# First expert stage: activations become the matmul weights, and the layout is put right by 32x32 transposes and a finer reload

## The chip, the cores and the metric

The kernel runs on one core of a Trainium2 chip. The time is device microseconds (us) of one execution, from runs on the chip; a profiled execution shows what each engine did. TensorE is called PE in the rows (PEld is its loading of weights), VectorE is DVE, ScalarE is ACT, GpSimd is POOL, and SP is SyncE, whose queue issues all the transfers of this kernel.

## The reference, cut to what matters

A gated linear recurrence over 4 batches, 8 heads, 768 steps and head size 40 gives 3072 tokens of 320 features. Two expert layers follow:

```
x = attn_out.transpose(0, 2, 1, 3).reshape(3072, 320)
h = maximum(x @ w1_in, 0);   x2  = (h * h) @ w1_out      # 320 -> 2048 -> 320
h = x2 @ w2_in;              out = (h * sigmoid(h)) @ w2_out
```

Inputs and output are float32. The kernel keeps that precision by splitting each factor into a high part and a low remainder and adding three products: high x high, high x low, low x high.

## The kernel before, in words

**Stages.** Stage 1 is the first expert layer in 8 blocks of 384 tokens (n = 0 to 7), with the recurrence (24 tiles of 128 tokens) woven in between; from the last blocks on it is alone. Stage 2 is the second layer in 6 blocks of 512 tokens. Each block has 16 steps j, one for each 128 of the 2048 hidden features. "Out step (n, j)" below is the second product of step j in block n, and "in step (n, j)" the first; blocks of stage 2 are n = 8 to 13.

**A step.** `in_mm` makes the hidden features with 8 matmuls into the PSUM tile `hin` (two buffers). ACT and DVE turn that into `gh` (high part) and `gl` (low part), 128 features by the tokens of the block. `emit_out` adds the second product into the PSUM tiles `o0`, `o1`, `o2` (and `o3` in stage 2), which have one buffer each, so the next block's out step 0 can't start until they have been copied out. In steps run three steps ahead of out steps (`AHEAD`).

**The two ways of the second product.** In stage 1 the weights `wo` are loaded into PE and `gh` and `gl` stream past: the result has features in rows and tokens in columns, which is what stage 2's first product needs. The 320 features are cut in 128, 128 and 64; the last 64 are laid beside their low parts, so that 8 matmuls of 384 columns do the step (lines 764 to 773). The two halves of the last tile are added later by POOL (line 811). In stage 2 `gh` and `gl` are loaded as the weights, 128 tokens at a time, and `wo` (320 columns) streams: 3 matmuls for each 128 tokens (lines 783 to 785).

**Between the stages.** ACT, DVE and ACT copy `o0`, `o1`, `o2` to `ob` (lines 776 to 778), and one transfer writes it to `x2_d` in DRAM. `x2_load` reads a block of 512 tokens back into `xr` (two buffers), in 5 transfers (lines 801 and 804), and `x2_split` makes the high part on ACT (line 812) and the low part on DVE (line 813). The first load is asked for at the start of block 7. In block 7 the weights of stage 2 are read back as well, 640 KB at a time (`w2_take`: `wi0`, `wo0`, `wi1`, ...), each when stage 1 is done with that weight tile.

**Order.** Block 0 follows a written table (`ORDER`). In blocks 1 to 7 the order of the code is the order on PE, ACT, DVE and SP. From block 8 on only PE's order is that of the code; the framework's own simulation places that work of the others, some of it (block 9's reload) in among block 7's, so a change of tiles moves it on ACT, DVE and SP. Each of these works through its list strictly in order: an instruction that waits holds up all behind it.

Of the kernel before, what the change touches and what calls it, by code (L numbers as in the profile page):

```python
# [8 lines left out]
F32 = mybir.dt.float32  # L9
F32R = mybir.dt.float32r  # L10
# [101 lines left out]
def f(ap):  # L112
    return ap.bitcast(F32)
# [7 lines left out]
def mlstm_moe_kernel(  # L121
# [32 lines left out]

    g_d = dram.tile([B * H, S], F32, name="g_d")
    e_d = dram.tile([B * H, S], F32, name="e_d")
    x2_d = dram.tile([128, 3, NT], F32, name="x2_d")
    w2_d = {(k, u): dram.tile([128, 1280], F32, name=f"w2{k}{u}_d") for u in range(8) for k in "io"}


# [112 lines left out]
    def w_split(raw, which, layer, u, pl):  # L273
        n = 768 if which == "i" else 640
        lo, hi = raw[:, :, 0], raw[:, :, 1]
        t = pl.tile([128, 768], I32, tag="dt", name="dt", bufs=DT_BUFS)[:, 0:n]
        act.activation(out=f(t), in_=f(hi), func=ACTF.Prelu, scale=2.0 ** -112, alpha=-2.0 ** 32)
        yield
        dve.tensor_scalar(out=t, in0=t, scalar1=3, scalar2=None, op0=ALU.logical_shift_left)
        dve.scalar_tensor_tensor(out=t, in0=lo, scalar=29, in1=t,  # L280
                                 op0=ALU.logical_shift_right, op1=ALU.bitwise_or)
        yield
        if which == "i":
            if layer == 1:
# [11 lines left out]
        elif layer == 1:  # L296
            w = wout[layer, u] = wp.tile([128, 2, 640], F32R, tag=f"wo{u}", name=f"wo{u}")
            tv = f(t).rearrange("p (j n) -> p j n", j=2)
            parts = ((slice(0, 256), slice(0, 256), slice(256, 512)),
                     (slice(256, 320), slice(512, 576), slice(576, 640)))  # L300
            for c, oh, ol in parts:
                act.activation(out=w[:, :, oh], in_=tv[:, :, c], func=ACTF.Copy)
            yield
            for c, oh, ol in parts:
                (pool if PLAN.get(f"@Mo{u}", 1) else dve).tensor_tensor(out=w[:, :, ol], in0=tv[:, :, c], in1=f(w[:, :, oh]), op=ALU.subtract)  # L305
        else:
            ws = pl.tile([128, 1280], F32R, tag="raw", name="ws", bufs=RAW_BUFS)
            w = ws.rearrange("p (j n) -> p j n", j=2)
# [443 lines left out]
    def emit_out(bi, j):  # L752
# [6 lines left out]
                O[bi].append(p_at.tile([128, 512], F32, tag="at", name="o3"))  # L759
        o = O[bi]  # L760
        first, last = j == 0, j == KF - 1
        if ly == 1:
            for k in range(2):
                c = slice(k * 128, k * 128 + 128)
                c2 = slice(256 + k * 128, 256 + k * 128 + 128)
                pe.matmul(o[k][:, 0:N], w[:, c], gh, start=first, stop=False)  # L766
                pe.matmul(o[k][:, 0:N], w[:, c2], gh, start=False, stop=False)  # L767
                pe.matmul(o[k][:, 0:N], w[:, c], gl, start=False, stop=last)  # L768
            if first:
                pe.matmul(o[2][:, 0:N], w[:, 512:640], gh, start=True, stop=False)  # L770
            pe.matmul(o[2][0:64, 0:N], w[:, 512:576], gl, start=False, stop=False)  # L771
            if not first:
                pe.matmul(o[2][:, 0:N], w[:, 512:640], gh, start=False, stop=last)  # L773
            if last:
                ob = stp.tile([128, 3, NMAX], F32, tag="raw", name="ob", bufs=RAW_BUFS)
                act.activation(out=ob[:, 0, 0:N], in_=o[0][:, 0:N], func=ACTF.Copy)
                dve.tensor_copy(out=ob[:, 1, 0:N], in_=o[1][:, 0:N])
                act.activation(out=ob[:, 2, 0:N], in_=o[2][:, 0:N], func=ACTF.Copy)
                late.append(lambda: sp.dma_start(out=x2_d[:, :, t0:t0 + N], in_=ob[:, :, 0:N]))
        else:  # L780
            for k in range(N // 128):
                c = slice(k * 128, k * 128 + 128)
                pe.matmul(o[k][:, 0:DM], gh[:, c], w[:, 0:320], start=first, stop=False)  # L783
                pe.matmul(o[k][:, 0:DM], gh[:, c], w[:, 320:640], start=False, stop=False)  # L784
                pe.matmul(o[k][:, 0:DM], gl[:, c], w[:, 0:320], start=False, stop=last)  # L785
            if last:
                ob = mp.tile([128, 4, DM], F32, tag="ob", name="ob")
                for k in range(N // 128):
                    if k % 2 == 0:
                        act.activation(out=ob[:, k], in_=o[k][:, 0:DM], func=ACTF.Copy)  # L790
                    else:
                        dve.tensor_copy(out=ob[:, k], in_=o[k][:, 0:DM])
                    b, c = TILES[t0 // L + k]
                    r0 = b * S + c * L
                    sp.dma_start(out=out[r0:r0 + L, :], in_=ob[:, k])

    def x2_load(n):
        ly, _, t0, N = blocks[len(BLK1) + n]
        xr = ph2.tile([128, 4, NMAX2], F32, tag="xr", name="xr", bufs=2)[:, :, 0:N]
        c = slice(t0, t0 + N)  # L800
        sp.dma_start(out=xr[:, 0:2], in_=x2_d[:, 0:2, c])
        for s in range(2):
            for p in range(2):
                sp.dma_start(out=xr[64 * p:64 * p + 64, 2 + s], in_=x2_d[64 * s:64 * s + 64, 2, c])
        return xr

    def x2_split(n, xr):
# [328 lines left out]
```

## Time and profile before

| | |
|---|---|
| median of 3 runs | 836.83 us (836.72 to 837.45) |
| profiled execution, its own time | 836.38 us |
| span of the profiled execution, first to last instruction | 834.7 us |
| PE busy | 828.2 us (99%) |
| DVE busy, ACT busy | 498.6 us (60%), 493.5 us (59%) |
| granted TensorE clock, mean | 0.999 |

The profiled execution lies 0.45 us below the median, and 1.7 us of it are outside the span. A matmul's busy time in the rows is longer than the distance to the next one's start, because matmuls are pipelined; what a group of matmuls costs is read from starts.

### The profile page before, as it was taken

What the parts mean: (1) busy time and instruction counts of PE and PEld (TensorE: products, weight loads), DVE (VectorE), ACT (ScalarE), POOL (GpSimd) and SP (SyncE); (2) the same over time, 40 slices, a digit from 0 to 9 for tenths busy, and PEclk for the clock granted to TensorE, in tenths of its full rate; (3) what the DMA queues carried; (4) which work ended last, traced back from release to release, by engine and by line L of the source; (5) the groups of instructions that cost most, each with busy time, mean ns of one, the idle gap of its engine ahead of it and who ended that gap; (6) DMA issues with size and microseconds to landing.
All of it is one profiled execution on the core that took longest, in us unless ns stands there. A gap on an engine that the chain in (4) does not pass through costs nothing.

```text
span 834.7 us, 14812 instructions
## 1 busy us (share of the span) xinstructions
PE 828.2 (99%) x5657; PEld 772.1 (92%) x5657; DVE 498.6 (60%) x904; ACT 493.5 (59%) x969; POOL 76.7 (9%) x102
## 2 busy tenths in 40 slices
PE   9999999999999999999999999999999999999998
PEld 5788999999999999999999989999999999999997
DVE  4689988687878776878843253443443533533433
ACT  4688877786977869779656653433333433433332
POOL 3242441100100000001000010000000000000000
PEclk9999999999999999999999999999999999999999
DMA  6777655667777668687511991020100000000000
GB/s 241 224 235 263 188 157 159 209 206 241 236 250 225 209 220 251 196 246 242 185 64 49 355 333 59 6 77 1 51 32 0 33 1 1 32 1 1 33 1 31
DMA packets 69454, 115.68 MB, mean 139 GB/s; under 512 B 5615, under 2 KB 47479, under 8 KB 69383
## 3 DMA queue, kind: packets, MB, share of 16 engines
q1 hardware_dynamic: 69383, 114.74, 42.8%
q8 instruction: 44, 0.72, 0.4%
q14 instruction: 27, 0.22, 0.1%
HBM read 75.48 MB, written 19.33 MB: 114 GB/s over the span
## 4 chain that ended last, share of the span: by engine, by line
PE 94%; DMA 2%; ACT 2%; SPq 1%; DVE 1%; issue 1%
PE hin L711 41%; PE o L785 7%; PE o L784 7%; PE o L783 7%; PE o L766 5%; PE o L767 5%; PE o L768 5%; PE o L771 3%; PE o L773 2%; PE hA L578 2%; PE sc L491 2%; PE hA L563 2%; PE st L613 1%; PE hA L573 1%; PE xT L647 1%; PE sc L485 1%
## 5 line engine op out<-in xcount | busy, mean ns | idle before, releaser
L711 PE MATMUL hin<-x,wi 128*128 128x384 f32 (+1 forms) x1792 | 395.2, 362 | 0.1
L711 PEld LDWEIGHTS hin<-x,wi 128*128 128x128 f32 x1792 | 320.9, 188 | 26.3 <-DVE wi L294 0.4
L742 DVE TENSOR_TENSOR gl<-r,gh 128x384 fp32r<-128x384 f32 (+1 forms) x224 | 140.3, 632 | 96.2 <-ACT gh L728 58.7
L728 ACT ACTIVATE gh<-r 128x384 fp32r<-128x384 f32 (+1 forms) x224 | 127.7, 571 | 69.9 <-DVE r L724 66.1
L724 DVE TENSOR_TENSOR r<-hin,r 128x512 f32<-128x512 f32 x96 | 66.4, 692 | 134.2 <-ACT r L723 134.2
L723 ACT ACTIVATE r<-hin 128x512 f32<-128x512 f32 x96 | 57.3, 597 | 144.8 <-PE hin L711 144.7
L785 PE MATMUL o<-wo,gl 128*128 128x320 f32 x384 | 118.7, 309 | 0.0
L784 PE MATMUL o<-wo,gh 128*128 128x320 f32 x384 | 118.5, 309 | 0.0
L783 PE MATMUL o<-wo,gh 128*128 128x320 f32 x384 | 118.2, 308 | 0.0
L721 ACT ACTIVATE r<-hin 128x384 f32<-128x384 f32 x128 | 62.0, 485 | 84.8 <-PE hin L711 80.9
L766 PE MATMUL o<-gh,wo 128*128 128x384 f32 x256 | 87.9, 343 | 0.0
L767 PE MATMUL o<-gh,wo 128*128 128x384 f32 x256 | 86.5, 338 | 0.0
L768 PE MATMUL o<-gl,wo 128*128 128x384 f32 x256 | 86.5, 338 | 0.0
L783 PEld LDWEIGHTS o<-wo,gh 128*128 128x128 f32 x384 | 72.1, 188 | 3.6
L784 PEld LDWEIGHTS o<-wo,gh 128*128 128x128 f32 x384 | 72.1, 188 | 3.6
L785 PEld LDWEIGHTS o<-wo,gl 128*128 128x128 f32 x384 | 72.1, 188 | 0.0
L736 ACT ACTIVATE r<-r 128x384 f32<-128x384 f32 x126 | 66.2, 525 | 3.8
L455 POOL TENSOR_SCALAR_AFFINE_SELECT W<-W 128x512 f32<-128x512 f32 x42 | 33.0, 807 | 262.8 <-DMA W<-g_d 96.0
L466 ACT ACTIVATE W<-W,aw 128x128 f32<-128x128 f32 x168 | 52.9, 389 | 0.1
L766 PEld LDWEIGHTS o<-gh,wo 128*128 128x128 f32 x256 | 48.1, 188 | 0.4 <-issue 0.2
L767 PEld LDWEIGHTS o<-gh,wo 128*128 128x128 f32 x256 | 48.1, 188 | 0.4 <-POOL wo L305 0.3
L768 PEld LDWEIGHTS o<-gl,wo 128*128 128x128 f32 x256 | 48.1, 188 | 0.0
(151 smaller groups left out, 995.9 us busy)
## 6 DMA issues: line engine op xcount, KB each, us to landing
stk<-tt SPq DMA_DIRECT2D x162, 120.0 KB
raw<-in_w_in_dram SPq DMA_DIRECT2D x16, 768.0 KB
W<-g_d SPq DMA_DIRECT2D x21, 512.0 KB
vk<-in_vk_dram SPq DMA_DIRECT2D x23, 328.0 KB
rqk<-in_qk_dram SPq DMA_DIRECT2D x18, 360.0 KB
ro<-in_w_out_dram SPq DMA_DIRECT2D x8, 640.0 KB
w2i_d<-ws SPq DMA_DIRECT2D x8, 640.0 KB
raw<-in_w_out_dram SPq DMA_DIRECT2D x8, 640.0 KB
```

The costliest lines, as they stand in the source:

```text
L711: pe.matmul(ps[:, 0:N], w[:, c, ws], x[:, sl, 0:N], start=(k == 0), stop=(k == 7))
L721: act.activation(out=r, in_=ps, func=ACTF.Relu)
L724: dve.tensor_tensor(out=r, in0=ps, in1=r, op=ALU.mult)
L728: act.activation(out=gh, in_=r, func=ACTF.Square if blocks[bi][0] == 1 else ACTF.Copy)
L736: act.activation(out=r, in_=r, func=ACTF.Square)
L742: on("gl" if ly == 1 else "gl2", gi).tensor_tensor(out=gl, in0=r, in1=f(gh), op=ALU.subtract)
L766: pe.matmul(o[k][:, 0:N], w[:, c], gh, start=first, stop=False)
L767: pe.matmul(o[k][:, 0:N], w[:, c2], gh, start=False, stop=False)
L768: pe.matmul(o[k][:, 0:N], w[:, c], gl, start=False, stop=last)
L783: pe.matmul(o[k][:, 0:DM], gh[:, c], w[:, 0:320], start=first, stop=False)
L784: pe.matmul(o[k][:, 0:DM], gh[:, c], w[:, 320:640], start=False, stop=False)
L785: pe.matmul(o[k][:, 0:DM], gl[:, c], w[:, 0:320], start=False, stop=last)
```

## The change: what it does

Stage 1's second product is now done as in stage 2: `gh` and `gl` are the weights, and `wo` streams with 320 columns, 9 matmuls for each out step of 384 tokens. The result has tokens in rows. At the end of a block three DVE instructions transpose each 32x32 block of `o0`, `o1`, `o2` on the way to `ob`. Three transfers write `ob` to `x2_d`, which now holds, for each 32 tokens, 32 rows of 320. The reload puts the blocks in their places with 12 transfers for each 512 tokens, each of 32 partitions by 16 pieces of 32 numbers (128 bytes); features 256 to 319 are read twice, as before. POOL's addition is gone. Stage 1's `w_out` is split with one ACT and one POOL or DVE instruction in place of two each.

```
-        if ly == 1:
-            for k in range(2):
-                c = slice(k * 128, k * 128 + 128)
-                c2 = slice(256 + k * 128, 256 + k * 128 + 128)
-                pe.matmul(o[k][:, 0:N], w[:, c], gh, start=first, stop=False)
-                pe.matmul(o[k][:, 0:N], w[:, c2], gh, start=False, stop=False)
-                pe.matmul(o[k][:, 0:N], w[:, c], gl, start=False, stop=last)
...
-                act.activation(out=ob[:, 0, 0:N], in_=o[0][:, 0:N], func=ACTF.Copy)
-                dve.tensor_copy(out=ob[:, 1, 0:N], in_=o[1][:, 0:N])
-                act.activation(out=ob[:, 2, 0:N], in_=o[2][:, 0:N], func=ACTF.Copy)
-                late.append(lambda: sp.dma_start(out=x2_d[:, :, t0:t0 + N], in_=ob[:, :, 0:N]))
...
+        for k in range(N // 128):
+            c = slice(k * 128, k * 128 + 128)
+            pe.matmul(o[k][:, 0:DM], gh[:, c], w[:, 0:320], start=first, stop=False)
+            pe.matmul(o[k][:, 0:DM], gh[:, c], w[:, 320:640], start=False, stop=False)
+            pe.matmul(o[k][:, 0:DM], gl[:, c], w[:, 0:320], start=False, stop=last)
+        if last and ly == 1:
+            ob = stp.tile([128, 3, NMAX], F32, tag="raw", name="ob", bufs=RAW_BUFS)
             for k in range(N // 128):
+                dve.transpose(out=ob[:, k, 0:DM], in_=o[k][:, 0:DM])
+            s0 = t0 // 32
+            late.append(lambda: [sp.dma_start(out=x2_d[s0 + 4 * k:s0 + 4 * k + 4].rearrange("s r d -> (s r) d"), in_=ob[:, k, 0:DM])
+                                 for k in range(N // 128)])
...
     def x2_load(n):
         ly, _, t0, N = blocks[len(BLK1) + n]
-        xr = ph2.tile([128, 4, NMAX2], F32, tag="xr", name="xr", bufs=2)[:, :, 0:N]
-        c = slice(t0, t0 + N)
-        sp.dma_start(out=xr[:, 0:2], in_=x2_d[:, 0:2, c])
-        for s in range(2):
-            for p in range(2):
-                sp.dma_start(out=xr[64 * p:64 * p + 64, 2 + s], in_=x2_d[64 * s:64 * s + 64, 2, c])
+        xr = ph2.tile([128, 3, NMAX2], F32, tag="xr", name="xr", bufs=2)[:, :, 0:N]
+        src = x2_d[t0 // 32:(t0 + N) // 32].rearrange("s r (b c) -> b r s c", c=32)
+        for k in range(12):
+            b = k if k < 10 else k - 2
+            p = 32 * (k % 4)
+            sp.dma_start(out=xr[p:p + 32, k // 4].rearrange("r (s c) -> r s c", c=32), in_=src[b])
         return xr
...
-        on("x2r").tensor_tensor(out=xr[:, 2], in0=xr[:, 2], in1=xr[:, 3], op=ALU.add)
-        act.activation(out=x[:, 0:3], in_=xr[:, 0:3], func=ACTF.Copy)
-        on("x2lo").tensor_tensor(out=x[:, 3:6], in0=xr[:, 0:3], in1=f(x[:, 0:3]), op=ALU.subtract)
+        act.activation(out=x[:, 0:3], in_=xr, func=ACTF.Copy)
+        on("x2lo").tensor_tensor(out=x[:, 3:6], in0=xr, in1=f(x[:, 0:3]), op=ALU.subtract)
```

The placing of stage 2's work moves with it. On SP's queue before, from the first reload (`xr_6323`, block 8's tokens) to the middle of the second one (`xr_6822`, block 9's); line numbers are those of each kernel's own file:

```order
L801 DMA xr_6323<-x2_d_86 128x2x512
L804 DMA xr_6323<-x2_d_86 64x512 x4
L316 DMA w2o7_d_102<-ws_6276 128x1280
L321 DMA wi0_6357<-w2i0_d_87 128x1280
L779 DMA x2_d_86<-ob_6311 384x1x384
...
L321 DMA wi2_6462<-w2i2_d_91 128x1280
L801 DMA xr_6822<-x2_d_86 128x2x512
L804 DMA xr_6822<-x2_d_86 64x512 x2
L324 DMA wo2_6488<-w2o2_d_92 128x1280
L321 DMA wi3_6514<-w2i3_d_93 128x1280
L804 DMA xr_6822<-x2_d_86 64x512 x2
```

And the same stretch of SP's queue now, where `xr_6431` and `xr_6956` are these two reloads:

```order
L785 DMA xr_6431<-x2_d_86 32x16x32 x12
L309 DMA w2o7_d_102<-ws_6382 128x1280
L314 DMA wi0_6473<-w2i0_d_87 128x1280
L765 DMA x2_d_86<-ob_6419 128x320 x3
...
L314 DMA wi3_6638<-w2i3_d_93 128x1280
L785 DMA xr_6956<-x2_d_86 32x16x32 x4
L317 DMA wo3_6665<-w2o3_d_94 128x1280
L314 DMA wi4_6692<-w2i4_d_95 128x1280
L785 DMA xr_6956<-x2_d_86 32x16x32 x8
```

A reload has 12 transfers in place of 5, and the last pieces of block 9's stand behind two more weight transfers, `wo3` and `wi4`.

On DVE at the end of block 7, before (`x_6996` is block 9's low part; `r` and `gl` of 512 columns belong to block 8; `ob_6752` is the copy of block 7's result):

```order
L813 TENSOR_TENSOR x_6996<-xr_6822,x_6996 128x1536
L724 TENSOR_TENSOR r_6687<-hin_6676,r_6687 128x512
L742 TENSOR_TENSOR gl_6660<-r_6661,gh_6659 128x384
L724 TENSOR_TENSOR r_6713<-hin_6702,r_6713 128x512
L742 TENSOR_TENSOR gl_6686<-r_6687,gh_6685 128x512
L724 TENSOR_TENSOR r_6739<-hin_6728,r_6739 128x512
L742 TENSOR_TENSOR gl_6712<-r_6713,gh_6711 128x512
L777 COPY ob_6752<-o1_6347 128x384
```

And DVE at the same place now:

```order
L717 TENSOR_TENSOR r_6816<-hin_6805,r_6816 128x512
L735 TENSOR_TENSOR gl_6788<-r_6789,gh_6787 128x384
L717 TENSOR_TENSOR r_6843<-hin_6832,r_6843 128x512
L735 TENSOR_TENSOR gl_6815<-r_6816,gh_6814 128x512
L793 TENSOR_TENSOR x_7137<-xr_6956,x_7137 128x1536
L717 TENSOR_TENSOR r_6870<-hin_6859,r_6870 128x512
L735 TENSOR_TENSOR gl_6842<-r_6843,gh_6841 128x512
L763 STREAM_TRANSPOSE ob_6884<-o0_6461 128x320
L763 STREAM_TRANSPOSE ob_6884<-o1_6462 128x320
L763 STREAM_TRANSPOSE ob_6884<-o2_6463 128x320
```

Block 9's low part (line 793) has moved behind block 8's second step, and stands three instructions ahead of the transposes that free `o0` to `o2` for block 8. ACT's high part for it (line 792) has moved with it, from ahead of block 7's last step to behind the sigmoid of step (8, 1).

## Rows read from the trace of the kernel before

**Rows 1.** The page, part 1: busy us (share of the span) xinstructions of each engine.

```profile
PE 828.2 (99%) x5657; PEld 772.1 (92%) x5657; DVE 498.6 (60%) x904; ACT 493.5 (59%) x969; POOL 76.7 (9%) x102
```

**Rows 2.** Waits of PE, longest first: first and last of the four.

```profile
PE warm L253 <- DVE wz L919: 1.1, 1, 1.1
...
PE xT L647 <- ACT cc L624: 0.5, 1, 0.5
```

**Rows 3.** Windows: stretch, length, busy us of engines, PEclk, DMA share, GB/s.

```profile
50.00:100.00 50.00, 49.90 (x338) 45.35 (x337) 46.53 (x90) 42.99 (x93) 15.27 (x15) 1.00 0.66 218
100.00:200.00 100.00, 99.49 (x858) 98.18 (x857) 80.13 (x159) 76.09 (x159) 20.29 (x21) 1.00 0.60 192
```

**Rows 4.** Timeline of PE, block 7: start us, us; out step (7, 2) and what follows.

```profile
452.61 0.33 PE L766 MATMUL o<-gh,wo 128*128 128x384 f32 x1
...
454.02 1.57 PE L711 MATMUL hin<-x,wi 128*128 128x384 f32 x8
```

**Rows 5.** Timeline of PE in stage 2: twelve matmuls of 320 columns, and what follows.

```profile
601.39 0.30 PE L783 MATMUL o<-wo,gh 128*128 128x320 f32 x1
...
603.14 2.00 PE L711 MATMUL hin<-x,wi 128*128 128x512 f32 x8
```

**Rows 6.** Groups of DVE by line and shape: the two copies out of PSUM.

```profile
L792 DVE COPY ob<-o 128x320 f32<-128x320 f32 x12 | 5.7, 487 | 3.8 <-PE o L785 3.8
...
L777 DVE COPY ob<-o 128x384 f32<-128x384 f32 x8 | 4.5, 557 | 3.3 <-PE o L768 3.1
```

**Rows 7.** Timeline, PE and DVE, where block 4 ends in stage 1.

```profile
338.17 0.34 PE L773 MATMUL o<-gh,wo 128*128 128x384 f32 x1
...
339.35 0.56 DVE L777 COPY ob<-o 128x384 f32<-128x384 f32 x1
...
339.76 0.33 PE L766 MATMUL o<-gh,wo 128*128 128x384 f32 x1
```

**Rows 8.** Timeline of SP's queue: the first two reloads and a weight transfer.

```profile
454.25 0.37 SPq L801 DMA_DIRECT2D xr<-x_d  x1
454.67 2.42 SPq L804 DMA_DIRECT2D xr<-x_d  x4
...
469.48 2.05 SPq L804 DMA_DIRECT2D xr<-x_d  x2
...
475.04 0.33 SPq L321 DMA_DIRECT2D wi<-w2i_d  x1
```

**Rows 9.** Timeline of POOL: the additions that wait for these reloads to land.

```profile
461.24 1.29 POOL L811 TENSOR_TENSOR xr<-xr 128x512 f32<-128x512 f32 x1 [65.75 <-DMA w2o_d<-ws]
481.33 1.29 POOL L811 TENSOR_TENSOR xr<-xr 128x512 f32<-128x512 f32 x1 [18.79 <-DMA xr<-x_d]
```

**Rows 10.** Windows: a 512-byte load, a reload, an output store, and block 7.

```profile
28.00:30.40 2.40, 2.40 (x23) 2.02 (x22) 2.17 (x8) 0.00 (x0) 0.74 (x2) 1.00 0.75 211
541.60:546.10 4.50, 4.50 (x27) 4.09 (x26) 1.72 (x3) 1.82 (x3) 0.00 (x0) 1.00 0.86 233
549.40:552.00 2.60, 2.60 (x16) 2.27 (x15) 1.26 (x4) 1.16 (x3) 0.00 (x0) 1.00 0.72 252
454.00:482.00 28.00, 28.00 (x163) 27.61 (x162) 7.16 (x11) 15.58 (x29) 1.97 (x2) 1.00 0.97 327
```

**Rows 11.** Timeline, PE, ACT and DVE, from in step (8, 0) to out step (8, 0).

```profile
481.96 2.01 PE L711 MATMUL hin<-x,wi 128*128 128x512 f32 x8
...
482.65 1.49 ACT L812 ACTIVATE x<-xr 128x1536 fp32r<-128x1536 f32 x1 [3.06 <-DMA wi<-w2i_d]
...
484.17 1.76 DVE L813 TENSOR_TENSOR x<-xr,x 128x1536 fp32r<-128x1536 f32 x1 [4.00 <-DMA wo<-w2o_d]
...
489.45 0.69 DVE L724 TENSOR_TENSOR r<-hin,r 128x512 f32<-128x512 f32 x1 [0.72 <-ACT r L723]
490.06 0.68 DVE L742 TENSOR_TENSOR gl<-r,gh 128x512 fp32r<-128x512 f32 x1
...
493.59 0.30 PE L783 MATMUL o<-wo,gh 128*128 128x320 f32 x1
```

More of the change, by code (lines that the diff above doesn't have):

```diff
@@ L156, in mlstm_moe_kernel @@
     e_d = dram.tile([B * H, S], F32, name="e_d")
-    x2_d = dram.tile([128, 3, NT], F32, name="x2_d")
+    x2_d = dram.tile([NT // 32, 32, DM], F32, name="x2_d")
     w2_d = {(k, u): dram.tile([128, 1280], F32, name=f"w2{k}{u}_d") for u in range(8) for k in "io"}
@@ L295, in w_split @@
             eng.tensor_tensor(out=w[64:128, 2], in0=tv[64:128, 2], in1=f(w[64:128, 2]), op=ALU.subtract)
[L296 to L305, printed above, removed]
-        else:
-            ws = pl.tile([128, 1280], F32R, tag="raw", name="ws", bufs=RAW_BUFS)
-            w = ws.rearrange("p (j n) -> p j n", j=2)
+        else:
+            if layer == 1:
+                w = wout[layer, u] = wp.tile([128, 2, 640], F32R, tag=f"wo{u}", name=f"wo{u}")
+            else:
+                ws = pl.tile([128, 1280], F32R, tag="raw", name="ws", bufs=RAW_BUFS)
+                w = ws.rearrange("p (j n) -> p j n", j=2)
             tv = f(t).rearrange("p (j n) -> p j n", j=2)
@@ L312, in w_split @@
             yield
-            dve.tensor_tensor(out=ol, in0=tv, in1=f(oh), op=ALU.subtract)
+            (pool if layer == 1 and PLAN.get(f"@Mo{u}", 1) else dve).tensor_tensor(out=ol, in0=tv, in1=f(oh), op=ALU.subtract)
         if layer == 2:
@@ L761, in emit_out @@
         first, last = j == 0, j == KF - 1
-        if ly == 1:
-            for k in range(2):
-                c = slice(k * 128, k * 128 + 128)
-                c2 = slice(256 + k * 128, 256 + k * 128 + 128)
-                pe.matmul(o[k][:, 0:N], w[:, c], gh, start=first, stop=False)
-                pe.matmul(o[k][:, 0:N], w[:, c2], gh, start=False, stop=False)
-                pe.matmul(o[k][:, 0:N], w[:, c], gl, start=False, stop=last)
[L769 to L775, printed above, removed]
-                act.activation(out=ob[:, 0, 0:N], in_=o[0][:, 0:N], func=ACTF.Copy)
-                dve.tensor_copy(out=ob[:, 1, 0:N], in_=o[1][:, 0:N])
-                act.activation(out=ob[:, 2, 0:N], in_=o[2][:, 0:N], func=ACTF.Copy)
-                late.append(lambda: sp.dma_start(out=x2_d[:, :, t0:t0 + N], in_=ob[:, :, 0:N]))
-        else:
-            for k in range(N // 128):
[L782 to L795, printed above, removed]
@@ new lines, in emit_out @@
+        for k in range(N // 128):
[5 more added lines that the diff above has]
+            ob = stp.tile([128, 3, NMAX], F32, tag="raw", name="ob", bufs=RAW_BUFS)
+            for k in range(N // 128):
+                dve.transpose(out=ob[:, k, 0:DM], in_=o[k][:, 0:DM])
+            s0 = t0 // 32
+            late.append(lambda: [sp.dma_start(out=x2_d[s0 + 4 * k:s0 + 4 * k + 4].rearrange("s r d -> (s r) d"), in_=ob[:, k, 0:DM])
+                                 for k in range(N // 128)])
+        elif last:
+            ob = mp.tile([128, 4, DM], F32, tag="ob", name="ob")
+            for k in range(N // 128):
+                if k % 2 == 0:
+                    act.activation(out=ob[:, k], in_=o[k][:, 0:DM], func=ACTF.Copy)
+                else:
+                    dve.tensor_copy(out=ob[:, k], in_=o[k][:, 0:DM])
+                b, c = TILES[t0 // L + k]
+                r0 = b * S + c * L
+                sp.dma_start(out=out[r0:r0 + L, :], in_=ob[:, k])
```

## The prediction, made before the result was known

> **What bounds the kernel now.** I read the page's busy shares first: PE is busy 99% of the span [rows 1]. A busy PE is not yet a PE that sets the time, so I read its waits next: four in all, the longest 1.1 us [rows 2]. The granted clock is 1.00 in the stretches of both windows, which is the 2.4 GHz level [rows 3]. So from the first microseconds on the time is the row of matmul starts, and what counts is the distance between starts. The other engines matter only where they would make PE wait: DVE is busy 46.5 of 50 us in block 0 and 80.1 of 100 us in block 1 [rows 3], and the DMA engines, idle in stage 2, have a share of 0.97 in block 7, while the stage-2 weights come back [rows 10].
>
> **The matmuls.** An out step of stage 1 lasts from 452.61 to 454.02, 1.41 us for 8 matmuls of 384 columns [rows 4]. In stage 2 twelve matmuls of 320 columns last from 601.39 to 603.14, 1.75 us or 0.1458 us each [rows 5]. These are the very form that stage 1 now gets, each with its own load of activations as weights, so 9 of them take 1.313 us. The step gains 0.097 us, and 8 blocks of 16 steps gain 128 x 0.097 = **12.4 us**. By columns alone (2880 for 3072) it would be 6.25% of 1.41 us, 11.3 us in all; I take the measured distances.
>
> Block 0 may not give its share, 16 x 0.097 = 1.55 us, since DVE there is full to 93% and its list is fixed. I take half as lost, **0.8 us** (bounds 0 and 1.55).
>
> `gl` now enters as a weight, and is needed after two matmuls as before, 0.06 us earlier. That costs nothing: in steps run three steps ahead, over 8 us, and this covers it. The merged splits of `w_out` and the two ACT copies that go away at each block's end save time on engines that PE doesn't wait for: nothing. So do POOL's six additions, except that they end a reload's chain, which is counted below.
>
> **The transposes.** Three DVE instructions replace one DVE and two ACT copies. No row has a transpose. The nearest is a copy of the same shape out of PSUM, 487 ns [rows 6], and that is my value and the lower bound; two such passes, 0.97 us, are the upper. The Vector Engine (DVE) Microarchitecture Reference of the Trainium skill (section 3.8) says that the transposing array is pipelined to one element per cycle and lane, which would give the copy's time; no run here shows it yet. A block's out step 0 may start one in step after the last matmul, 1.41 us or so. Where DVE is free it can begin with `o0` while PE works on `o1` and `o2`, and is done in time even at 0.97 us. Where block 4 ends it is late: the last out matmul starts at 338.17, DVE's copy at 339.35, and the next block's first matmul into `o0` at 339.76 [rows 7]. Transposes from 339.35 would free `o0`, `o1`, `o2` at 339.84, 340.33 and 340.82, against wants at 339.76, then 0.44 us apart: about 0.2 us lost (1.7 us at 0.97). DVE's next work there, a score tile, moves by 0.9 us; I allow **0.3 us** for all seven ends within stage 1 (0 to 3).
>
> **The reload.** This is the disputed part. A load of 512 tokens was 5 transfers and 512 pieces of 2 KB; it is now 12 transfers and 12 x 512 = 6144 pieces of 128 bytes. What a piece costs I get from two windows with one kind of traffic each: 1024 pieces of 512 bytes (one load of `W`, 128 partitions by 8 heads), 0.75 x 2.40 us x 16 engines / 1024 = 28 ns; 512 pieces of 1280 bytes (the output of four tiles), 0.72 x 2.60 x 16 / 512 = 58 ns [rows 10]. The line through both gives 13 ns at 128 bytes. So a load takes 6144 x 13 / 16 = 5.0 us of all engines (lower bound); if a small piece costs as much as one of 512 bytes, 10.8 us (upper). It takes 0.86 x 4.50 = 3.9 us now. I take 5.5 us, near the line, a little over it because block 7's traffic is dense.
>
> When must it be there? The first reload starts at 454.25, just behind out step (7, 2); call that T0 [rows 4, 8]. Block 8's data are wanted by ACT some ten steps later, about T0 + 19; even the upper bound, with twelve issues of 0.6 us as the four of 2.42 us show [rows 8], is in time. The second reload is the tight one. Before, its addition on POOL started at 481.33, T0 + 27.1 [rows 9], and ACT had already waited 3.06 us for it, without harm to PE [rows 11]. Now its last eight transfers stand behind two more weight transfers on SP. At 327 GB/s for a share of 0.97, 640 KB take 1.95 us, so 3.9 us for both. Both reloads lie in this saturated stretch, so each adds its own growth: landing at T0 + 27.1 + 3.9 + 2 x (5.5 - 3.9) = T0 + 34.2.
>
> The want has moved too. The low part of block 9 now precedes, on DVE, the transposes that free `o0` for out step (8, 0). That step started at 493.59, T0 + 39.3 [rows 11]; 13 out steps shorter by 0.097 us bring it to T0 + 38.1. From landing to a free `o0` lie the high part on ACT 1.49, the low part on DVE 1.76, one product 0.69 and one `gl` 0.68 [rows 11], and a transpose 0.49: 5.1 us. So the data are wanted at T0 + 33.0, and PE waits 34.2 - 33.0 = **1.2 us**. With 5.0 us a load it is 0.2; with 10.8 us, 11.8.
>
> Later reloads have a block of some 57 us for themselves, and the DMA engines are nearly idle: nothing. The two extra issues of `x2_d` writes per block cost SP about a microsecond, behind which stand transfers for tiles several us off: nothing; without that slack, as much again per block, at most 8 us.
>
> **The sum** against the profiled execution: 836.4 - 12.4 + 0.8 + 0.3 + 1.2 = 826.3 us. That execution is 0.45 us below the median of the runs; I say **826.6 us**.
>
> **The rivals.**
>
> *Small pieces cost what 512-byte pieces cost.* Then a load takes 10.8 us, ACT stands at block 9's high part, DVE behind it, the transposes behind that, and PE waits 11.8 us at out step (8, 0): 836.8 - 12.4 + 0.8 + 0.3 + 11.8 = 837.3, no change. For it: the share of 0.97 leaves no slack in block 7, and no row has a piece near 128 bytes. Against it: the two windows show a cost that falls with size. The page "DMA: Bandwidth & Descriptors" of the Trainium skill (Specifications) says that below 512 bytes a transfer misses line rate because of a read-modify-write; by that rule the time would be this rival's, and no run before shows whether it holds for reads from DRAM.
>
> *The same place, but dearer pieces: slower.* At 40 ns a piece, a strided read of DRAM being unlike the contiguous rows, a load takes 15.4 us and the wait is 2 x 4.6 = 9.2 us longer than that: 846.5. Slower begins where the wait passes 13 us, at 11.4 us a load or 30 ns a piece. Against it: 28 ns were enough for four times the bytes.
>
> *DVE becomes the bound in stage 1.* It gains 24 x 0.487 - 8 x 0.557 = 7.2 us there, just where blocks begin with a burst of its work, and transposes at 0.97 us would add 12 more. PE would wait some 0.5 us at each of 8 ends: about 830. Against it: DVE has a fifth of its time free in block 1.
>
> *The change doesn't shorten the product at all.* If the loads of activations as weights (they are new for every matmul) set the distance in stage 1, the gain is gone and the reload still costs: 838. Against it: stage 2 runs the same form at 0.1458 us.
>
> **How the numbers follow.** The forecast with a reload wait up to 4 us, 823.5 to 829.5: 0.60. A wait of 4 to 8 us, up to 834: 0.14. The 512-byte cost, 834 to 838.5: 0.12, half of it still faster by over 0.2%. Dearer pieces: 0.08. DVE as the bound: 0.04. No shorter product: 0.02. 0.2% (1.7 us) is about what a measurement of this kernel can tell from no change. Faster: 0.60 + 0.14 + 0.06 + 0.04 = 0.84; same: 0.06 + 0.02 = 0.08; slower 0.08. The range 823.8 to 834.5 leaves out some 0.05 below and 0.15 above. The forecast's own range is 823.5 to 829.5.
>
> **What would show it.** Right: out steps of stage 1 at 1.31 us between starts; transposes near 0.49 us; PE's waits still under 3 us outside the end of block 7, and there one wait of 0 to 4 us before out step (8, 0) put down to the transposes or, behind them, to the second reload; a span near 824.6. Wrong: the packets of 128 bytes well above 15 ns each and ACT idle for many us ahead of block 9's high part (the reload rivals); or DVE transposes near 1 us with a wait of PE at each block's end; or distances of 320-column matmuls above 0.15 us in stage 1.

## The result, and the profile after

The changed kernel takes 829.66 us (median of 6 runs, 828.98 to 831.38) against 836.85 us of the kernel before on the same chip: a ratio of 0.9908, 95% interval 0.9888 to 0.9928. The forecast was 826.6 us, faster. The profiled execution took 828.98 us, its span 827.0 us; the span before was 834.7 us, so 7.7 us are to be found in the trace.

The page, part 1, of the kernel after, for [rows 1]:

```profile
PE 819.4 (99%) x5785; PEld 767.1 (93%) x5785; DVE 505.5 (61%) x916; ACT 487.3 (59%) x945; POOL 66.2 (8%) x92
```

PE has 128 matmuls more (one for each out step) and is busy for less. The longest waits of PE after (us in total, times, longest), for [rows 2]:

```profile
PE warm L253 <- DVE wz L899: 1.1, 1, 1.1
PE sc L484 <- DMA stk<-tt: 0.7, 1, 0.7
PE xT L640 <- ACT cc L617: 0.7, 1, 0.7
PE o L757 <- ACT gh L721: 0.5, 1, 0.5
```

The first three were there before, at 1.1, 0.5 and 0.5 us; the second lies in block 1, the third at the end of block 4. The fourth is new, the one ahead of out step (8, 0). The windows of [rows 3] after (busy us of PE, PEld, DVE, ACT, POOL; PEclk; DMA share; GB/s):

```profile
50.00:100.00 50.00, 49.76 (x354) 45.51 (x353) 47.81 (x86) 42.97 (x88) 14.49 (x13) 1.00 0.65 213
100.00:200.00 100.00, 99.23 (x902) 98.96 (x901) 84.25 (x167) 74.82 (x155) 19.09 (x20) 1.00 0.62 193
```

PE's clock is granted in full as before, and DVE is fuller by 1.3 and 4.1 us. Out step (7, 2) and the in steps behind it, PE's timeline (start us, us), for [rows 4]:

```profile
445.08 0.31 PE L757 MATMUL o<-wo,gh 128*128 128x320 f32 x1
...
446.40 1.55 PE L704 MATMUL hin<-x,wi 128*128 128x384 f32 x8
...
473.64 2.00 PE L704 MATMUL hin<-x,wi 128*128 128x512 f32 x8
```

The out step is 1.32 us, before 1.41. The ten steps from the second row to the third take 27.24 us; before, the same ten took 27.94 (454.02 to 481.96, [rows 4, 11]).

**Where the 7.7 us come from.** I follow both kernels' out steps in PE's timeline and take, at the end of each block, how much earlier the changed kernel is. The first out step begins 0.48 us later than before; at the end of block 0 the gain is 0.13 us, then 1.28, 2.63, 3.95, 5.10, 6.05, 7.39 and, at the end of block 7, 8.63. Behind out step (8, 0) it is 7.87, and 7.7 at the end of the span. The out steps of a block became shorter by 1.36, 1.35, 1.34, 1.35, 1.24, 1.36 and 1.28 us in blocks 1 to 7, and by 1.02 in block 0. Where a block's gain is smaller than that, a gap ahead of some step grew.

The transposes, DVE's groups by line and shape (busy us, mean ns), for [rows 6]:

```profile
L763 DVE STREAM_TRANSPOSE ob<-o 128x320 f32<-128x320 f32 x24 | 10.7, 498 | 0.2
...
L773 DVE COPY ob<-o 128x320 f32<-128x320 f32 x12 | 5.7, 487 | 3.8 <-PE o L759 3.8
```

A transpose costs what the copy costs. The Vector Engine (DVE) Microarchitecture Reference of the Trainium skill (section 3.8) says of the transposing array that it is pipelined to one element per cycle and lane, by which it would cost the copy's time; the trace agrees (498 ns for 487). The end of block 4, PE and DVE, for [rows 7]:

```profile
333.10 0.31 PE L759 MATMUL o<-wo,gl 128*128 128x320 f32 x1
333.25 1.56 PE L704 MATMUL hin<-x,wi 128*128 128x384 f32 x8
...
334.34 1.31 DVE L763 STREAM_TRANSPOSE ob<-o 128x320 f32<-128x320 f32 x3
...
334.91 0.42 PE L757 MATMUL o<-wo,gh 128*128 128x320 f32 x1
```

DVE is late, as before, and block 5's first out step starts 1.66 us after its in step, 0.25 us more than before; the step itself is 0.11 us longer than its neighbours, since `o1` and `o2` come one by one. That makes 0.36 us.

The two reloads on SP's queue, for [rows 8]:

```profile
446.64 6.16 SPq L785 DMA_DIRECT2D xr<-x_d  x12
...
460.99 6.57 SPq L785 DMA_DIRECT2D xr<-x_d  x4
467.66 3.21 SPq L317 DMA_DIRECT2D wo<-w2o_d  x1
...
471.40 6.64 SPq L785 DMA_DIRECT2D xr<-x_d  x8
```

T0 is 446.64. Two windows in which a reload is read (columns as above, the last two the DMA share and GB/s); in the second no other transfer is issued:

```profile
446.60:453.50 6.90, 6.90 (x44) 6.90 (x43) 1.68 (x3) 3.43 (x8) 0.00 (x0) 1.00 0.66 104
530.00:540.00 10.00, 10.00 (x57) 8.99 (x56) 5.46 (x7) 4.17 (x7) 0.00 (x0) 1.00 0.47 74
```

104 GB/s for 6.90 us are 5606 pieces of 128 bytes, and 74 GB/s for 10 us 5781: 0.66 x 6.90 x 16 / 5606 = 0.47 x 10 x 16 / 5781 = 13.0 ns of one engine a piece, as the line through the two windows of before had said. The page "DMA: Bandwidth & Descriptors" of the Trainium skill (Specifications) speaks of a read-modify-write below 512 bytes; in these reads a piece of 128 bytes costs less than half of the 28 ns of one of 512, so they do not show it.

From the second reload to out step (8, 0), ACT, DVE and PE (in brackets the wait before a row, and what ended it), for [rows 11]:

```profile
480.63 1.49 ACT L792 ACTIVATE x<-xr 128x1536 fp32r<-128x1536 f32 x1 [1.19 <-DMA xr<-x_d]
...
482.15 1.76 DVE L793 TENSOR_TENSOR x<-xr,x 128x1536 fp32r<-128x1536 f32 x1 [1.39 <-ACT x L792]
...
483.82 0.68 DVE L717 TENSOR_TENSOR r<-hin,r 128x512 f32<-128x512 f32 x1
484.43 0.68 DVE L735 TENSOR_TENSOR gl<-r,gh 128x512 fp32r<-128x512 f32 x1
...
485.02 1.30 DVE L763 STREAM_TRANSPOSE ob<-o 128x320 f32<-128x320 f32 x3
...
485.63 0.38 PE L757 MATMUL o<-wo,gh 128*128 128x320 f32 x1 [0.53 <-ACT gh L721]
```

This is the chain of the prediction, row by row. The data land at 480.63 (ACT's start), T0 + 34.0, and out step (8, 0) starts 5.0 us later. The wait is put down to ACT's `gh`, but PE starts some 0.1 us after the first of the three transposes can be done (485.02 + 0.50): it is `o0` that came last.

### The profile page after: what moved, and what is told of

Read it like the earlier page. It is cut to its first block, busy times and chain, and to the rows that moved or that the text cites. A ratio compares the mean times of both kernels' runs of the same rounds, so it can differ in the third digit from the quotient of the medians.

```text
span 827.0 us, 15126 instructions
## 1 busy us (share of the span) xinstructions
PE 819.4 (99%) x5785; PEld 767.1 (93%) x5785; DVE 505.5 (61%) x916; ACT 487.3 (59%) x945; POOL 66.2 (8%) x92
## 4 chain that ended last, share of the span: by engine, by line
PE 89%; DMA 3%; SPq 2%; ACT 2%; issue 2%; DVE 1%; POOL 0%; ACTq 0%; DVEq 0%
PE hin L704 40%; PE o L757 13%; PE o L758 13%; PE o L759 13%; PE hA L571 2%; PE sc L484 2%; PE hA L556 2%; PE st L606 1%; DMA raw<-in_w_in_dram 1%; PE xT L640 1%; SPq L785 1%; DMA sg<-in_og_dram 1%; PE hA L566 1%; DMA rqk<-in_qk_dram 0%; SPq L443 0%
## 5 line engine op out<-in xcount | busy, mean ns | idle before, releaser
L757 PE MATMUL o<-wo,gh 128*128 128x320 f32 x768 | 239.1, 311 | 0.6 <-ACT gh L721 0.5
L758 PE MATMUL o<-wo,gh 128*128 128x320 f32 x768 | 237.4, 309 | 0.2 <-POOL wo L306 0.2
L759 PE MATMUL o<-wo,gl 128*128 128x320 f32 x768 | 237.2, 309 | 0.0
L757 PEld LDWEIGHTS o<-wo,gh 128*128 128x128 f32 x768 | 144.2, 188 | 5.3 <-ACT gh L721 0.9
L758 PEld LDWEIGHTS o<-wo,gh 128*128 128x128 f32 x768 | 144.3, 188 | 4.2 <-POOL wo L306 0.5
L759 PEld LDWEIGHTS o<-wo,gl 128*128 128x128 f32 x768 | 144.2, 188 | 0.0
L279 DVE TENSOR_SCALAR dt<-dt 128x768 int32<-128x768 int32 (+1 forms) x32 | 17.3, 541 | 18.0 <-ACT dt L277 17.8
L505 DVE TENSOR_TENSOR pr<-W 128x512 f32<-128x512 f32 x36 | 26.5, 735 | 1.2
L506 DVE TENSOR_TENSOR p<-pr 128x512 bf16<-128x512 f32 x36 | 26.3, 732 | 1.2
L499 DVE TENSOR_TENSOR W<-sc,W 128x512 f32<-128x512 f32 x36 | 24.5, 682 | 3.3 <-issue 1.6
L277 ACT ACTIVATE dt<-raw 128x768 f32<-128x768 f32 (+1 forms) x24 | 20.8, 866 | 3.4 <-DMA raw<-in_w_in_dram 2.5
L280 DVE SCALAR_TENSOR_TENSOR dt<-raw,dt 128x768 int32<-128x768 int32 (+1 forms) x24 | 22.3, 927 | 0.8
```

## The experiments

All are compared with the kernel before on the same chip. "Reloads in the order of the code" below means one edit, which is shown at the experiment of that name. The gain of a kernel is always how much earlier it is than the kernel before, in PE's timeline.

**The changed kernel once more**, to see how the waits vary.

> The changed kernel itself once more, beside the three below, so that they have a kernel of the same hour to stand against. Theory (10.6 us gained by the distances of the matmuls, some 2.7 us given back in waits of PE): 829.7 us, and the same waits of PE as in its first profile: about 0.2 us at block 4's end and 0.7 us ahead of out step (8, 0). If the waits in blocks 0 and 1 (about 1.3 us) are chance of that one execution, they will be different here.

829.58 us (828.84 to 829.94), ratio 0.9913 (0.9898 to 0.9927). PE's longest wait in this execution, and ACT's and PE's rows for it:

```profile
PE o L757 <- ACT gh L721: 1.6, 1, 1.6
```

```profile
481.60 1.49 ACT L792 ACTIVATE x<-xr 128x1536 fp32r<-128x1536 f32 x1 [2.26 <-DMA xr<-x_d]
...
486.61 0.38 PE L757 MATMUL o<-wo,gh 128*128 128x320 f32 x1 [1.60 <-ACT gh L721]
```

The same place, but 1.6 us in place of 0.5. The gain ahead of out step (8, 0) was 8.73 us, behind it 6.91: 1.8 us lost there. The data landed later, at T0 + 35.1 (T0 is 446.54 here), and the step again started 5.0 us behind them. So the size of this wait is a matter of the execution: it hangs on when the transfers land. Block 0's gain was the same (0.14 us); the loss in block 1 was not there.

**A coarse reload.** It reads whole 2 KB pieces and leaves out the putting of the blocks in their places.

```
-        src = x2_d[t0 // 32:(t0 + N) // 32].rearrange("s r (b c) -> b r s c", c=32)
-        for k in range(12):
...
+        src = x2_d[t0 // 32:(t0 + N) // 32].rearrange("s r d -> (s r) d").rearrange("(p q) d -> p (q d)", q=4)
+        for k, c in enumerate((0, 512, 768)):
+            sp.dma_start(out=xr[:, k], in_=src[:, c:c + N])
```

> The reload alone undone: 3 transfers of 128 pieces of 2 KB for each 512 tokens in place of 12 of 512 pieces of 128 bytes (the numbers then stand in wrong places, nothing else is left out). Theory: the reload costs only PE's wait of 0.7 us ahead of out step (8, 0), so that wait goes and the time is 0.8 us less than the changed kernel's, 828.9 us. Rival (the crowding by small pieces in block 7 and behind it took the missing gain): 2 to 3 us less, about 827 us.

828.04 us (827.39 to 828.95), ratio 0.9893 (0.9876 to 0.9909). There is no wait ahead of out step (8, 0): the gain is 7.98 us ahead of it and 7.99 behind. (Block 0 lost 0.6 us more in this execution, by a wait for `wo`.) It is 1.5 us faster than the changed kernel on the same chip, between what theory (0.8) and rival (2 to 3) gave, since the wait itself varies from 0.8 to 1.8. The fine reload costs the changed kernel that wait and elsewhere nothing that shows. This run doesn't tell small pieces from the order of work: its second reload is also asked for earlier (455.94 in place of 460.99), and block 9's low part stands at 470.16 on DVE, ahead of all of block 8. The runs with reloads in the order of the code and with half the piece tell them apart.

**Copies in place of transposes.**

```
-                dve.transpose(out=ob[:, k, 0:DM], in_=o[k][:, 0:DM])
+                dve.tensor_copy(out=ob[:, k, 0:DM], in_=o[k][:, 0:DM])
```

> The transposes alone undone: the same three DVE instructions per block as plain copies (so the blocks stay untransposed). Theory: a transpose costs what a copy costs (510 ns against 487), so the time is the changed kernel's within 0.4 us, 829.7 us. Rival (DVE's transposes hold up the tiles of the recurrence and took the missing gain): 2 us less, about 827.7 us.

829.29 us (829.08 to 829.46), ratio 0.991 (0.9895 to 0.9925), and the waits stay where they were (1.0 us ahead of out step (8, 0), which starts 5.0 us behind a landing at T0 + 34.5). A copy takes 488 ns where the transpose takes 498. That an instruction transposes costs nothing here that shows.

**Reloads in the order of the code.** ACT, DVE and SP keep the code's order through block 8 as well, where block 9's reload stands behind block 8's first steps.

```
-                if bi in (1, nb1):
+                if bi in (1, nb1 + 1):
```

> Only the placing of work is changed: ACT, DVE and SP keep the order of the code through block 8 as well, so that block 9's high and low parts stand behind the transposes of block 7 and not ahead of them. Theory: PE's wait ahead of out step (8, 0) came from that order (the second reload's landing, its high part, its low part, then the transposes), so it goes: 0.7 us less than the changed kernel, 829.0 us. Rival (the wait is the transposes' own time, three in a row on one engine with one PSUM buffer each): it stays at 0.5 us or more, 829.6 us.

828.01 us (827.71 to 828.05), ratio 0.9894 (0.988 to 0.9909); the fastest version of this study with the whole work in it, faster than both kernels, and 1.6 us below the changed one on the same chip. Its SP, DVE and PE:

```profile
485.34 13.33 SPq L785 DMA_DIRECT2D xr<-x_d  x24
```

```profile
483.42 1.31 DVE L763 STREAM_TRANSPOSE ob<-o 128x320 f32<-128x320 f32 x3
```

```profile
484.48 0.30 PE L757 MATMUL o<-wo,gh 128*128 128x320 f32 x1
```

The second reload starts at 485.34, behind the transposes, and out step (8, 0) waits for nothing (gain 9.10 ahead of it, 9.11 behind). The pieces are as small as in the changed kernel: the wait came from the order. The order moves the second reload out of block 7 too; that its traffic is not the cause, the run with half the piece shows. The time fell by 1.6 us and not by the 0.7 of the first profile's wait, as the wait is longer in other executions.

**The product alone.** The coarse reload, and ACT, DVE and ACT copy the tiles out.

```
-                dve.transpose(out=ob[:, k, 0:DM], in_=o[k][:, 0:DM])
+                if k == 1:
+                    dve.tensor_copy(out=ob[:, k, 0:DM], in_=o[k][:, 0:DM])
+                else:
+                    act.activation(out=ob[:, k, 0:DM], in_=o[k][:, 0:DM], func=ACTF.Copy)
```

> The product change alone: no transposes (ACT, DVE and ACT copy the three tiles out, as before the change) and the reload in 3 transfers of 2 KB pieces, so the numbers of the second stage stand in wrong places. Theory: the product gives 128 x 0.0825 = 10.6 us, and what is missing beyond that is lost in blocks 0, 1 and 4, not in the transposes or the reload; out step (8, 0) does not wait: 836.8 - 10.6 + 1.5 = 827.7 us (826.9 to 828.6). Rival: the product gives the 12.4 us of the prediction, and the transposes and the reload take 2 to 3 of them even where no wait shows: 825.0 to 826.0 us.

827.46 us (827.00 to 832.01), ratio 0.9883 (0.9854 to 0.9911), span 825.6. The out steps of blocks 1 to 7 are shorter by 9.4 us, hardly more than the 9.3 of the changed kernel, and the product alone saves 9.1 us of span. So the 12.4 us of the prediction aren't there even where nothing has to be put right, and what is missing is in the steps themselves. Block 4's end in PE's timeline:

```profile
338.45 1.56 PE L704 MATMUL hin<-x,wi 128*128 128x384 f32 x8
339.85 0.31 PE L757 MATMUL o<-wo,gh 128*128 128x320 f32 x1
```

1.40 us and no wait, against 1.66 above; block 5 gives its 1.34 us in full. So the 0.36 us there are the price of doing all three on DVE, transposed or not (the kernel with three copies has the wait too).

**A narrower stream**, 256 columns, with reloads in the order of the code; features 256 to 319 are left out.

```
+            m = 256 if ly == 1 else 320
-            pe.matmul(o[k][:, 0:DM], gh[:, c], w[:, 0:320], start=first, stop=False)
+            pe.matmul(o[k][:, 0:m], gh[:, c], w[:, 0:m], start=first, stop=False)
...
```

> The changed kernel with reloads in the order of the code through block 8, and the second product of stage 1 streams 256 columns in place of 320: features 256 to 319 are left out of it and of the write, and the reload reads others in their place. Theory: a matmul costs 13.3 ns and 0.4167 ns for each column (from distances of 146.7, 173.3 and 226.7 ns at 320, 384 and 512 columns), so 256 columns take 120.0 ns, an out step 1.08 us in place of 1.32, 0.24 us less: 828.0 - 128 x 0.24 = 797.3 us; block 0 may keep its share, 3.8 us, since DVE there is full (796.5 to 801.5). Rival, cost by columns alone (0.458 ns each): 117.3 ns, an out step of 1.056 us and 828.0 - 33.8 = 794.2 us. Rival, the loads of activations as weights set the distance: no change, 828 us.

809.16 us (808.72 to 812.08), ratio 0.9664 (0.9632 to 0.9695): 18.9 us below the version with reloads in the order of the code, where 30.7 or 33.8 were expected. Most out steps did become that short, 1.05 to 1.07 us, nearer the 1.056 of a price by columns alone than the 1.08 of a fixed part. But PE now waits:

```profile
PE sc L484 <- DMA stk<-tt: 6.9, 8, 1.6
PE hA L571 <- DVE p L506: 3.0, 4, 1.1
```

In blocks 1 to 5 the out steps are shorter than before by 5.6 us a block, and the gaps longer by 2.3 to 3.4. By these waits the recurrence's chain, through the transfers of `stk` and DVE, bounds stage 1 there. In block 7, first and last of eight in steps (PE):

```profile
438.25 1.55 PE L704 MATMUL hin<-x,wi 128*128 128x384 f32 x8
...
455.47 2.00 PE L704 MATMUL hin<-x,wi 128*128 128x512 f32 x8
```

17.22 us for 7 steps, 2.460 each. The rival of the loads is out. By whole steps the other two lie too near each other to be told apart (8 x 173.3 ns and 9 matmuls of 120.0 or 117.3 make 2.466 or 2.442).

**Halved matmuls.** The same columns in 18 matmuls for 9 in out steps 1 to 14 of each block, with reloads in the order of the code.

```
+            m = 160 if ly == 1 and 0 < j < KF - 1 else 320
+            for g, e in ((gh, 0), (gh, 320), (gl, 0)):
+                for q in range(0, DM, m):
+                    pe.matmul(o[k][:, q:q + m], g[:, c], w[:, e + q:e + q + m], start=first and g is gh and e == 0, stop=last and g is gl)
```

> The changed kernel with reloads in the order of the code through block 8, and in out steps 1 to 14 of each block of stage 1 each matmul of 320 columns is done as two of 160, with its weights loaded twice: the same columns in 18 matmuls in place of 9. Theory of the fixed part: 160 columns take 13.3 + 66.7 = 80.0 ns, the step 1.44 us in place of 1.32, and 8 x 14 x 0.12 = 13.4 us are added: 841.4 us (840 to 843). Rival, cost by columns alone: 1.32 us a step and 828.0 us. Rival, 160 columns are too short to hide the next load of weights (the page's mean busy time of one load is 772.1 us / 5657 = 136 ns): 18 x 0.136 = 2.46 us a step, 1.14 us more, 955 us.

902.45 us (901.82 to 903.57), ratio 1.077 (1.0732 to 1.0809). A halved step, PE's timeline:

```profile
512.51 1.59 PE L704 MATMUL hin<-x,wi 128*128 128x384 f32 x8
513.93 0.57 PE L760 MATMUL o<-wo,gh 128*128 128x160 f32 x4
...
515.90 1.60 PE L704 MATMUL hin<-x,wi 128*128 128x384 f32 x8
```

513.93 to 515.90 is 1.97 us, 109 ns for each matmul, and 112 steps longer by 0.65 us are 73 of the 74 us that it is slower by. Neither of the first two theories holds; the third does in kind, at 109 ns in place of 136. I read that as the price of a load of 128 columns of weights when it stands free. The issuing of matmuls and loads doesn't take that long: the recurrence's 48 bf16 matmuls of 42 columns, each with a load of its own, start 25 ns apart in the kernel before (line 578's window: length, PE, PEld, PEclk, DMA share, GB/s):

```profile
404.23:405.44 1.21, 1.21 (x48) 1.21 (x48) 1.00 0.38 126
```

"TensorE: Matmul & The Clock Gate" of the Trainium skill (LDWEIGHTS) says columns / 1.2 in ns, by which it would be 107 ns; the trace agrees (109 ns). Matmuls of 320 columns take longer than that (147 ns) and hide it.

**Half the piece.** 24 transfers of 64-byte pieces for a load. Block 9's high and low parts come to stand behind the transposes here.

```
...
+            for h in range(2):
+                sp.dma_start(out=xr[p:p + 32, k // 4].rearrange("r (s h c) -> r h s c", h=2, c=16)[:, h], in_=src[b, h])
```

> The changed kernel with each of the 12 transfers of a reload cut into two, of 64-byte pieces: 24 transfers and 12288 pieces for 512 tokens. The scheduler puts block 9's high and low parts much later in block 8 here, behind the transposes of block 7's end. Theory of the order (the wait ahead of out step (8, 0) comes from block 9's low part standing ahead of the transposes, not from the traffic itself): no wait there although the second reload lands 10 to 20 us later, 828.2 us (827.4 to 829.2). Rival, the traffic of small pieces itself holds up PE, by way of the weights that come back in block 7: twice the pieces cost at least what the wait in the changed kernel cost again, 831 to 842 us.

833.66 us (830.77 to 838.12), ratio 0.9955 (0.9937 to 0.9974). Out step (8, 0) has no wait, as the theory of the order says (gain 8.26 ahead of it, 8.27 behind). But the time is the rival's, for a reason of neither: the wait moved on. PE's longest wait, and ACT's row ahead of it:

```profile
PE hin L704 <- DVE r L717: 4.4, 1, 4.4
```

```profile
505.64 1.48 ACT L793 ACTIVATE x<-xr 128x1536 fp32r<-128x1536 f32 x1 [7.29 <-DMA xr<-x_d]
```

The data land at T0 + 58.6 (T0 is 447.01 here). ACT stands for 7.29 us at block 9's high part, and everything of block 8 behind it. Windows of this kernel (columns as above: PEclk, the granted clock, is the third from the end), and PE's in steps:

```profile
498.00:502.00 4.00, 4.00 (x24) 3.57 (x23) 0.69 (x1) 0.34 (x1) 0.00 (x0) 1.00 0.94 325
...
506.00:510.00 4.00, 0.43 (x1) 0.44 (x2) 2.36 (x2) 2.06 (x3) 0.00 (x0) 0.79 0.92 213
510.00:514.00 4.00, 4.00 (x12) 3.23 (x12) 1.99 (x3) 1.85 (x4) 0.00 (x0) 0.50 0.88 159
```

```profile
501.44 2.00 PE L704 MATMUL hin<-x,wi 128*128 128x512 f32 x8
509.56 3.78 PE L704 MATMUL hin<-x,wi 128*128 128x512 f32 x8 [4.37 <-DVE r L717]
515.81 2.00 PE L704 MATMUL hin<-x,wi 128*128 128x512 f32 x8
```

The step from 501.44 takes 8.12 us, where the one ahead of it took 3.59 (in steps stand at 497.85 and 501.44). After the wait the clock stands at 0.50, the 1.2 GHz level, and the next step takes 6.25 us. So a wait of 4.4 us cost 7.2: the gain fell from 8.27 to 1.09 us. The shorter waits of the changed kernel leave the clock at 1.00. The executions of this kernel vary with their mean granted clock, from 0.989 at 838.12 us to 1.0 at 830.77.

**A wider stream**, 384 columns of `w_out`'s tile, with reloads in the order of the code; the product with its low parts is left out.

```
+            m, e = (384, 0) if ly == 1 else (320, 320)
...
+            pe.matmul(o[k][:, 0:m], gh[:, c], w[:, e:e + m], start=False, stop=False)
...
```

> The changed kernel with reloads in the order of the code through block 8, and each of the 9 matmuls of an out step of stage 1 streams 384 columns of w_out's tile (its low parts are left out). Read in block 7's stretch without recurrence, from one in step's first matmul to the next one's (before 2.794 us with 8 + 8 matmuls of 384 columns, the changed kernel 2.724 with 8 + 9 of 384 and 320, the narrow one 2.460 with 256): if 384 columns cost the same in either form, 17 matmuls at 2.794 / 16 = 174.6 ns give 2.969 us. Rival, activations as weights cost more at any width (0.4577 ns a column, as in the changed and in the narrow kernel): 0.4577 x 6528 = 2.988 us, or more where the second product alone carries the difference: 2.724 + 9 x 64 x 0.459 = 2.989 us. By 13.3 ns and 0.4167 ns a column it would be 17 x 173.3 = 2.947 us. Time: 828 + 128 x 0.25 = 860 us (857 to 863).

857.39 us (2 runs), ratio 1.0234 (1.0217 to 1.0252). In steps (6, 15), (7, 5), (7, 7) and (7, 11), PE:

```profile
452.08 1.55 PE L704 MATMUL hin<-x,wi 128*128 128x384 f32 x8
...
469.96 1.55 PE L704 MATMUL hin<-x,wi 128*128 128x384 f32 x8
...
475.89 1.55 PE L704 MATMUL hin<-x,wi 128*128 128x384 f32 x8
...
487.67 1.55 PE L704 MATMUL hin<-x,wi 128*128 128x384 f32 x8
```

2.980 us a step over the first six, which end ahead of the stretch of the expectation's 2.794, and 2.945 over the last four, which lie in it: 175.3 and 173.2 ns a matmul. In that stretch it is the 2.947 of 13.3 ns and 0.4167 ns a column, a little below the theory's 2.969, and the 2.988 of dearer activations is out. Ahead of it the kernel before takes 2.82 us a step (out steps (7, 1) to (7, 2)), which would make 2.996 for 17 matmuls; 2.980 is no dearer either.

**The kernel before with a shorter stream**, 320 tokens in out steps 1 to 14; the last 64 tokens of a block are left out of them.

```
+            m = N if first or last else 320
-                pe.matmul(o[k][:, 0:N], w[:, c], gh, start=first, stop=False)
+                pe.matmul(o[k][:, 0:m], w[:, c], gh[:, 0:m], start=first, stop=False)
...
```

> The kernel before, with the 8 matmuls of out steps 1 to 14 of each block of stage 1 streaming 320 tokens in place of 384 (the last 64 tokens of a block are left out of these steps). From one in step to the next in block 7: if 320 columns cost the same in either form, 8 x 174.6 + 8 x 147.5 ns = 2.577 us (147.5 being (2.724 - 8 x 0.1746) / 9). Rival, w_out as weights costs less at any width, 0.4548 ns a column: 0.4548 x 5632 = 2.561 us. Time: 836.8 - 112 x 0.23 = 811 us if the other engines keep up, and up to 15 us more, as the narrow kernel lost in the blocks with the recurrence.

816.15 us (2 runs), ratio 0.9742 (0.9725 to 0.9759). In steps of block 7, PE:

```profile
431.74 1.57 PE L711 MATMUL hin<-x,wi 128*128 128x384 f32 x8
...
457.55 1.57 PE L711 MATMUL hin<-x,wi 128*128 128x384 f32 x8
```

25.81 us for ten, 2.581 each, where the same cost in either form gives 2.577 and cheaper `w_out` weights 2.561. What is loaded and what streams makes no difference that shows; the number of columns and of matmuls does. The time lies 5 us above the 811 of engines that keep up, within what the expectation allowed; PE's longest waits are now 1.5 us for DVE and 1.4 us ahead of an `sc` matmul.

**The kernel before with reloads in the order of the code.**

```
-                if bi in (1, nb1):
+                if bi in (1, nb1 + 1):
```

> The kernel before, with ACT, DVE and SP kept in the order of the code through block 8. Theory: the 1.6 us that this order gave the changed kernel were the wait ahead of out step (8, 0), which the kernel before doesn't have: no change, 836.8 us (836.2 to 837.4). Rival: the order of the code is better in itself, and the change owes nothing to that wait: 835.2 us.

836.54 us (836.08 to 840.72), ratio 0.9991 (0.9981 to 1.0001), span 834.7 as before. The order of the code gives the kernel before nothing that can be measured; it gives the changed one 1.6 us because there it takes the wait away.

## Why the prediction was right, and where its sum was off

Direction and range (823.8 to 834.5) held; the narrower one of the forecast itself, 823.5 to 829.5, was missed by 0.2 us. The sum fell short by 3.1 us (829.66 for 826.6). Against its own profiled execution (826.3 forecast, 828.98 measured) it was off by 2.7:

| term | forecast us | measured us |
|---|---|---|
| matmuls, all 8 blocks | -12.4 | -10.7 |
| block 0's share lost | +0.8 | +1.2 |
| transposes at a block's end | +0.3 | +0.36 |
| wait ahead of out step (8, 0) | +1.2 | +0.76 |
| gaps in blocks 1 and 4 | 0 | +0.4 |
| small gaps, behind (8, 0) and outside the span | 0 | +0.6 |

**The matmuls: the term that was mis-sized.** Blocks 1 to 7 became shorter by 9.27 us in their out steps, 9.38 without the 0.11 of the transposes; with 1.34 for block 0, as for the others, that is 10.7, or 0.084 us a step and not 0.097. "1.41 us for 8 matmuls" was read from one step, (7, 2), and "0.1458 us each" from stage 2. Of the 112 out steps in blocks 1 to 7, the 89 usual ones take 1.38 to 1.41 us before and 1.31 to 1.33 after, on average 1.405 and 1.321. So a matmul of 320 columns costs 0.1468 us in stage 1, where stage 2 gave 0.1458: that is 0.008 us a step and some 1.0 of the 1.7 us, and the 1.41 that is 1.405 is most of the rest. The prediction's other way, by columns alone, 11.3 us, was nearer: 0.4587 ns a column at 320 and 0.4573 at 384. From out step (7, 3) on ten steps are 1.38 us before and 1.31 after, a gain of 0.07; there the price from stage 2 was right and the 1.41 was wrong, but that is only 0.1 us of the sum. The product alone shows that the missing part is no loss to the reload or the transposes, and the wide and the short stream that it is not the activations as weights. Why the same kernel's steps differ between stretches (1.41 and 1.38, 1.32 and 1.31) stays open.

**Block 0.** Its gain is 0.13 of some 1.34 us, so 1.2 are lost, within the bounds of 0 and 1.55. They lie in the start (0.48 later), a `wo` that POOL delivers 0.2 us late, and gaps of 0.40; the gain at its end varies from -0.46 to 0.63 us among the executions of this study with the new product at 320 columns. The prediction's reason was DVE's full list. No run shows that as the cause: of these losses only a `wi` that DVE delivers 0.2 us late is a wait for DVE, and the start varies as much among executions. The half was a guess.

**The transposes** came out as worked out, at block 4's end and nowhere else. DVE did not become the bound. The narrower stream shows how near that is: with a product shorter by another 4 us a block, the recurrence's chain takes back 2.3 to 3.4 us in each of blocks 1 to 5.

**The reload** was forecast at T0 + 34.2 and landed at T0 + 34.0, and from there to out step (8, 0) it took 5.0 us for 5.1. Three executions with this order (the second with copies in place of transposes) landed at T0 + 34.0, 34.5 and 35.1, and each time the step started 5.0 us behind: the chain is the prediction's. PE lost 0.76, 1.2 and 1.8 us by it. Pieces cost 13 ns, so both rivals of dear pieces fall. The order of the code takes the wait away, twice the pieces behind the transposes bring none ahead of out step (8, 0), and the kernel before gains nothing by the order: the wait's cause is shown. That the landing was met within 0.2 us is luck in part. With 13 ns, a load of 5.0 us and not 5.5, the same sum gives T0 + 33.2; and it takes the DMA engines to be full up to the landing. Their share (second number from the end) was 0.90:

```profile
446.60:480.60 34.00, 34.00 (x207) 33.23 (x206) 9.45 (x15) 20.09 (x36) 0.00 (x0) 1.00 0.90 256
```

Some 3 us of them were not used, so the sum holds errors that go opposite ways. What a later landing can do shows in the kernel with half the piece: a PE wait of 4.4 us grew to 7.2 by the clock, a price that the prediction's sums of waits left out.

**Not forecast:** 0.2 us each in block 1 (a wait for `stk`) and at the last out step of block 4 (a tile's `xT` waits for ACT, 0.7 us for 0.5). The first was not lost in the second execution; the other came in every run with 320 columns. It may be that PE now arrives earlier at work that doesn't come earlier; no run shows it.

## What to carry to other kernels

Take the price of a step from a dozen of them, in the stretch where the change applies: the prediction's prices came from one step and from the other stage, and 0.013 us a step were 1.7 us of the sum. A layout that must be put right costs little if the eviction does it on the way (498 ns for 487) and the reload has a block's time; look then for the one reload that has not, and at what stands behind it on the engines that wait for it. A scheduler that places work by its own estimate may put such a wait ahead of something urgent: writing the order out was worth 1.6 us here, as much as the coarse reload gave.

## What the runs showed of the hardware

Matmuls of 160 columns that each load 128 columns of fp32 weights start 109 ns apart, and the load did not show with 256 columns (117 to 118 ns) or more. 128-byte pieces read from DRAM cost 13 ns of one engine each; what makes a reload long on the queue is the 12 issues of some half a microsecond (6.16 us). One PE wait of 4.4 us brought the granted clock to 0.50 for a step behind it and cost 2.8 us on top, while waits of up to 1.6 us left it at 1.00.
